# Moving one MLP step behind a division, and two v loads from slot 6 to slot 8

## The chip, the cores and the metric

The kernel runs on one core of one Trainium2 chip. Times are microseconds (us) on the device, from the first to the last instruction and what lies around them. A core has five engines that run beside each other, each in its own fixed order: PE (TensorE, matmuls; its weight loads are shown as PEld), DVE (VectorE), ACT (ScalarE), POOL (GpSimd) and SP (SyncE, which here only issues transfers). POOL issues the loads that also convert from 32 to 16 bits; SP issues stores, on-chip copies and DMA transposes. All transfers run on the same 16 DMA engines.

## The reference

Two stages. First a causal attention with a forget gate, 8 batches of 8 heads, 576 rows, head width 64; then an MLP of 512 to 2048 to 512 on all 4608 rows, with g = h - tanh(h) between.

```
scores = scale * np.matmul(q, k.transpose(0, 1, 3, 2))
log_f = np.log(np.clip(f, 0.0001, 1.0))
cum = np.cumsum(log_f, axis=-1)
decay = cum[:, :, :, None] - cum[:, :, None, :]
scores = np.where(causal, -1000000000.0, scores + decay)
attn = np.exp(scores - np.max(scores, axis=-1, keepdims=True))
attn = attn / (np.sum(attn, axis=-1, keepdims=True) + 1e-09)
x = np.matmul(attn, v) ...   # heads put side by side: (4608, 512)
h = x @ w_in
out = (h - np.tanh(h)) @ w_out
```

## The kernel before

**Order.** Every engine executes the program's order as it is written; no scheduler moves anything. The attention runs by pairs of heads, 4 pairs in each of the 8 batches. Batch 0 is written out by hand by blocks of 128 rows (0 to 3, and block 4 of 64 rows). From batch 1 on, a loop runs over slots: slot p (from 4) is the pair p of the list of (batch, pair), so slots 4 to 7 are batch 1, 8 to 11 batch 2, 12 to 15 batch 3. A slot has 7 tiles of scores. Between the tiles stand the loads of LOADS, keyed by (slot, tile), the transposes of TRANS, and, after tile 1, the value matmuls and the division of the pair of the slot before. MLP steps are put between these as filler for PE: `step()` emits the next one from a list. The first 13 are first-layer steps of unit 0, which are 8 matmuls of 256 columns each (L468), a tanh on ACT (L434) and an add on DVE (L435).

**Batch 0, by hand.** `scores0(ib, ti)` makes one tile of scores of block ib (L319, L322) and its exponential on ACT (L324); the score tiles use two PSUM banks in turn, so a tile waits for the exponential of the last but one. `values0(ib, halves)` multiplies the exponentials with v (L334). `norm0(ib)` divides on DVE (L343 to L345). `turn0(ib)` transposes the divided block on PE (L354) and copies it to XR (L355), where the MLP reads it. `trans(1, 0, qn, QT)` and `trans(1, 0, kn, KT)` transpose batch 1's first q and k on PE (L262) and copy them, half on ACT (L269) and half on DVE (L271). Steps, block 3's transpose and k's transposes share three further PSUM banks in turn.

**Loads.** `load_v(b, n)` (L94) loads block n of batch b's v, for all heads, into `vn[b % 2]`. `load_heads` (L105) loads block n of q or k of a batch from 3 on into a raw buffer; `turn_all` then transposes the whole raw buffer into TQ or TK with one DMA transpose on SP (L108), and `place` (L112) copies it to QT or KT. `weight_sums` (L458) are sums of parts of w_out for a fast product of the later units; the second group is written into raw q's buffer after TQ has read it. Each mask of a score tile is a select on POOL (L397), in the same queue as the loads, and the value matmuls (L406) wait for the masks. `load_wout` (L211) loads w_out in four parts. The loads on POOL use eight semaphores in turn: a load waits until the eighth load before it has landed.

**Who reads what.** Batch 2's v is read first by the values of its first pair, in slot 9 after tile 1. TQ of batch 3 is issued at (8, 4), TK at (9, 4), and batch 3's scores begin in slot 12.

Of the kernel before, what the change touches and what calls it, by code (L numbers as in the profile page):

```python
# [17 lines left out]
FAR = 3  # L18
# [4 lines left out]
def kernel(  # L23
# [54 lines left out]
    raw = [[qkp.tile([P, RW], FP16, tag=f"{x}n{i}", name=f"{x}n{i}") for i in range(2)] for x in "qk"]  # L78
# [13 lines left out]
    def load_block(dst, src, b, n, h0=0, h1=H):  # L92
        pn = min(P, S - n * P)
        nc.gpsimd.dma_start(out=dst[0:pn, n, h0:h1, 0:D], in_=src[b, h0:h1, n * P:n * P + pn, :].rearrange("h p d -> p h d"))  # L94
# [6 lines left out]
    def load_heads(dst, src, b, n):  # L101
        pn = min(P, S - n * P)
        to = dst[0:pn, n * P:n * P + D]
        to = bass.AP(to.tensor, to.offset, [list(to.ap[0]), [HP, H], [1, D]])
        nc.gpsimd.dma_start(out=to, in_=src[b, :, n * P:n * P + pn, :].rearrange("h p d -> p h d"))  # L105

    def turn_all(dst, src):
        nc.sync.dma_start_transpose(out=dst.rearrange("p (x t) -> p x t", t=P), in_=src[:, 0:TC])  # L108

    def place(dst, src, b, a):  # L110
        of = src[a * D:(a + 1) * D, a * LEAD:a * LEAD + NPAIR * PITCH].rearrange("d (c s) -> d c s", s=PITCH)
        nc.sync.dma_start(out=dst[b % 2][0:D, a:H:2, 0:S], in_=of[:, :, 0:S])  # L112

    def load_v(b, n):
        load_block(vn[b % 2], v, b, n)

    def raw_of(b):
        return 1 if b == FAR else 0
# [50 lines left out]
    def load_aug(b):  # L169
        i, h0 = b % 2, b * H  # L170
        nc.sync.dma_start(out=KT[i][D:D + 1, :, 0:S], in_=chi[h0:h0 + H, :])
        nc.sync.dma_start(out=QT[i][D + 2:D + 3, :, :], in_=cq[h0:h0 + H, :])
        nc.sync.dma_start(out=KT[i][D + 1:D + 2, :, 0:S], in_=clo[h0:h0 + H, :])
# [40 lines left out]
    def load_qk(dst, src, b, h0, h1):  # L214
        nc.gpsimd.dma_start(
            out=dst[b % 2][:, h0:h1, :, :].rearrange("p h n d -> p h (n d)"),
            in_=src[b, h0:h1, :, :].rearrange("h (p n) d -> p h (n d)", n=NT6))

    LOADS = {(NPAIR, 5): [lambda: load_qk(qn, q, 2, 0, HH)],
             (NPAIR + 1, 2): [lambda: load_qk(kn, k, 2, 0, HH)],  # L220
             (NPAIR + 1, 4): [lambda: load_qk(qn, q, 2, HH, H)],
             (NPAIR + 1, 6): [lambda: load_qk(kn, k, 2, HH, H)]}
# [6 lines left out]
    for b in range(2, B):  # L229
        p0 = (b - 1) * NPAIR  # L230
        for n in range(NJ):
            LOADS.setdefault((p0 + (2 if b == 2 else 1), n), []).append(lambda b=b, n=n: load_v(b, n))
        LOADS.setdefault((p0, 0), []).append(lambda b=b: load_aug(b))
        if b < FAR:
            continue
        for n in range(NJ):
            LOADS.setdefault((p0 - 1, n), []).append(lambda b=b, n=n: load_heads(raw[0][raw_of(b)], q, b, n))
            LOADS.setdefault((p0, n), []).append(lambda b=b, n=n: load_heads(raw[1][raw_of(b)], k, b, n))
        LOADS.setdefault((p0, 4), []).append(lambda b=b: turn_all(TQ, raw[0][raw_of(b)]))
        LOADS.setdefault((p0 + 1, 4), []).append(lambda b=b: turn_all(TK, raw[1][raw_of(b)]))  # L240
        for n, (dst, src) in enumerate(((QT, TQ), (KT, TK))):
            for a in range(2):
                LOADS.setdefault((p0 + 1 + n, 5 + a), []).append(lambda b=b, dst=dst, src=src, a=a: place(dst, src, b, a))
# [9 lines left out]
    def trans(b, c, src, dst, eng):  # L253
        pn, g3 = S // NT6, NT6 // 2
        if src is kn and (b, c) <= (2, 0):
            t32 = ps_m.tile([P, UW], FP32, tag="m", name="t32")
        else:
            t32 = ps_tr.tile([P, UW], FP32, tag="tr", name="t32")
        t16 = t32.bitcast(FP16)[:, 0:2 * S // 2].rearrange("p (a g n) -> p a g n", a=2, g=g3)
        for a in range(2):  # L260
            for g in range(g3):
                nc.tensor.transpose(out=t16[:, a, g, :],  # L262
                                    in_=src[b % 2][:, 2 * c + a, 2 * g:2 * g + 2, :],
                                    identity=id16[0:pn, 0:pn])
        for e in range(2):
            to = dst[b % 2][0:D, 2 * c:2 * c + 2, e:S:2].rearrange("d a (p g) -> d a p g", g=g3)
            of = t16[e * D:(e + 1) * D, :, :, :].rearrange("d a g p -> d a p g")
            if eng[e] == "A":
                nc.scalar.activation(out=to, in_=of, func=AF.Copy)  # L269
            else:  # L270
                nc.vector.tensor_copy(out=to, in_=of)  # L271
# [39 lines left out]
    def scores0(ib, ti):  # L311
        w = min(P, S - ib * P)
        n = UW // w
        ps = ps_sc.tile([P, 512], FP32, tag="sc", name="ps")
        e = aex.tile([P, 512], FP16, tag="e", name="e")
        todo = [(h, j) for h in range(H) for j in range(ib + 1)][n * ti:n * ti + n]
        for i, (h, j) in enumerate(todo):
            at = slice(i * w, (i + 1) * w)
            nc.tensor.matmul(out=ps[:, at], lhsT=KT[0][:, h, j * P:(j + 1) * P],  # L319
                             rhs=QT[0][:, h, ib * P:ib * P + w], start=True, stop=(j < ib))  # L320
            if j == ib:
                nc.tensor.matmul(out=ps[:, at], lhsT=neg16, rhs=tri16[:, 0:w], start=False, stop=True)  # L322
            E[(0, h, j, ib)] = e[:, at]
        nc.scalar.activation(out=e, in_=ps, func=AF.Exp, scale=qscale)  # L324

    def values0(ib, halves=(0, 1)):
        w = min(P, S - ib * P)
        if ib not in AV:
            av = ps_av.tile([P, 2, 512], FP32, tag="av", name="av")
            AV[ib] = av[0:w, :, 0:HH * (D + 1)].rearrange("p i (h d) -> p i h d", h=HH)  # L330
        av = AV[ib]
        for h in [a * HH + x for a in halves for x in range(HH)]:
            for j in range(ib + 1):
                nc.tensor.matmul(out=av[:, h // HH, h % HH, :], lhsT=E.pop((0, h, j, ib)),  # L334
                                 rhs=vn[0][:, j, h, 0:D + 1], start=(j == 0), stop=(j == ib))

    def norm0(ib):
        w = min(P, S - ib * P)
        av = AV.pop(ib)
        xn = fin.tile([P, NJ, P], FP16, tag="xn", name="xn")  # L340
        XN[(0, ib)] = xn[0:w, 0:NPAIR, :]
        rs = fin.tile([P, 2, HH, 1], FP32, tag="rs0", name="rs")[0:w]
        nc.vector.tensor_scalar_add(out=rs, in0=av[:, :, :, D:D + 1], scalar1=1e-9)  # L343
        nc.vector.reciprocal(out=rs, in_=rs)
        nc.vector.tensor_tensor(out=XN[(0, ib)].rearrange("p (i c) (a d) -> p i (c a) d", i=2, a=2),  # L345
                                in0=av[:, :, :, 0:D], in1=rs.to_broadcast([w, 2, HH, D]), op=ALU.mult)

    def turn0(ib):
        w = min(P, S - ib * P)
        xn = XN.pop((0, ib))  # L350
        x32 = ps_m.tile([P, UW], FP32, tag="m", name="x32")
        xt = x32.bitcast(FP16)[:, 0:NPAIR * w].rearrange("p (c n) -> p c n", c=NPAIR)
        for c in range(NPAIR):
            nc.tensor.transpose(out=xt[:, c, :], in_=xn[:, c, :], identity=id16[0:w, 0:w])  # L354
        nc.vector.tensor_copy(out=XR[:, :, ib * P:ib * P + w], in_=xt)  # L355
# [262 lines left out]
    def step(n=1):  # L618
        for fn, *args in mlp[done[0]:done[0] + n]:
            fn(*args)  # L620
        done[0] += n
# [132 lines left out]
    for _, two in raw:  # L754
        rows = two[3 * P // 4:P, 0:TC].rearrange("p (s d) -> p s d", d=D)
# [7 lines left out]
    scores0(3, 7)  # L763
    values0(3, (0,))
    scores0(4, 0)
    step()
    scores0(4, 1)
    values0(3, (1,))
    norm0(3)
    scores0(4, 2)  # L770
    trans(1, 0, qn, QT, "AV")
    turn0(3)
    scores0(4, 3)
    trans(1, 0, kn, KT, "AV")
    scores0(4, 4)
    step()
# [38 lines left out]
```

## Time and profile before

| what | us |
|---|---|
| median of 3 runs | 343.23 |
| lowest and highest of them | 342.43 and 344.86 |
| the profiled execution | 341.56 |
| its span, first to last instruction | 339.8 |
| DVE busy in the span | 238.3 (70%) |
| ACT busy | 226.5 (67%) |
| POOL busy | 162.2 (48%) |

The profile is one execution, recorded instruction by instruction. Busy times of different engines overlap. A matmul's recorded length includes the time that it takes to pass through the array, so one starts before the last has ended, and a busy PE can still lose time: the starts tell more than the lengths. L and a number is a line of the kernel; `out<-in` names what an instruction writes and reads; `x8` says that eight like it stand together. The landing of a transfer is the time at which its semaphore has its full count. The largest groups of POOL's loads on the page:

```profile
vn<-in_v_dram POOLq DMA_DIRECT2D x32, 128.0 KB, 6.9
...
qn<-in_q_dram POOLq DMA_DIRECT2D x24, 128.0 KB, 5.9
kn<-in_k_dram POOLq DMA_DIRECT2D x24, 128.0 KB, 4.4
```

(count, size, median us from issue to landing). In the slots of the change, slot 6 runs from about 46.5 us, slot 7 from 53, slot 8 from 60.5, slot 9 from 70 and slot 10 from 80.

### The profile page before, as it was taken

The page shows a single profiled execution, that of the slowest core. Times are in us where ns is not written, and L with a number is a line of the kernel's source. Part 1 is how long each engine was busy: PE and PEld are TensorE (multiplying, and loading weights), DVE is VectorE, ACT ScalarE, POOL GpSimd, SP SyncE. Part 2 cuts the span into 40 slices and gives each one's busy share as a digit, 9 for nine tenths or more (in the row PEclk, how much of TensorE's full clock was granted, in tenths as well). Part 3 has the DMA queues.
Part 4 walks back from the last instruction along what each step waited for, and adds up shares of the span by engine and source line. Part 5 has one row for each costly group of instructions (what it writes and reads, how often), then busy time and mean ns, then how long its engine had stood idle before and what let it go on. Part 6 is the DMA issues. An engine that isn't in the chain of part 4 may idle for free.

```text
span 339.8 us, 8818 instructions
## 1 busy us (share of the span) xinstructions
PE 330.9 (97%) x3405; PEld 237.8 (70%) x3405; DVE 238.3 (70%) x492; ACT 226.5 (67%) x424; POOL 162.2 (48%) x324
## 2 busy tenths in 40 slices
PE   7898999999999999999999999999999999999995
PEld 4887876655588558888885578657877786486484
DVE  7777884748985886478845885588547865974973
ACT  5787877778855886488557865787568734624731
POOL 8978387853466727772786358652222210000000
PEclk9999999999999999999999999999999999999999
DMA  9999999999999999999999999997230013012002
GB/s 85 148 195 185 206 190 166 178 150 208 189 134 113 207 207 126 154 229 180 152 133 207 183 155 158 196 179 172 62 112 19 20 50 110 1 33 93 2 31 93
DMA packets 162955, 45.96 MB, mean 135 GB/s; under 512 B 141602, under 2 KB 162402, under 8 KB 162914
## 3 DMA queue, kind: packets, MB, share of 16 engines
q0 software_dynamic: 101248, 18.36, 77.3%
q1 hardware_dynamic: 61586, 26.99, 39.1%
q8 instruction: 26, 0.43, 0.5%
q14 instruction: 15, 0.12, 0.1%
q10 hardware_dynamic: 80, 0.07, 0.1%
HBM read 36.85 MB, written 9.44 MB: 136 GB/s over the span
## 4 chain that ended last, share of the span: by engine, by line
PE 79%; DMA 11%; POOL 6%; issue 1%; DVE 1%; ACT 1%; POOLq 0%; ACTq 0%
PE hps L482 30%; PE cx L523 17%; PE cz L523 12%; PE ps L378 10%; PE av L406 7%; DMA wout<-in_moe_w_out_dram 5%; DMA vn<-in_v_dram 4%; PE ops L601 3%; DMA win<-in_moe_w_in_dram 2%; POOL vn L94 2%; POOL kn L98 1%; POOL qn L98 1%; POOL wout L211 1%; PE hps L468 1%; PE t L262 0%
## 5 line engine op out<-in xcount | busy, mean ns | idle before, releaser
L435 DVE TENSOR_TENSOR gt<-hps,th 128x512 f16<-128x512 f32 x144 | 98.7, 689 | 44.0 <-ACT th L434 42.9
L482 PE MATMUL hps<-XR,win 128*128 128x512 f16 (+4 forms) x640 | 125.8, 336 | 0.4 <-DVE gt L435 0.4
L387 ACT ACTIVATE e<-ps 128x512 f16<-128x512 f32 x168 | 98.4, 595 | 34.4 <-PE ps L378 33.2
L434 ACT ACTIVATE th<-hps 128x512 f32<-128x512 f32 x144 | 86.1, 598 | 28.0 <-PE hps L482 19.9
L397 POOL TENSOR_SCALAR_AFFINE_SELECT e<-e 128x128 f16<-128x128 f16 x162 | 55.1, 342 | 100.8 <-ACT e L387 100.4
L482 PEld LDWEIGHTS <-win 128*128 128x128 f16 x640 | 56.3, 97 | 43.8 <-issue 0.6
L378 PE MATMUL ps<-QT,KT 67*128 67x512 f16 (+1 forms) x336 | 68.6, 277 | 0.4 <-ACT e L387 0.3
L523 PEld LDWEIGHTS <-gt 128*128 128x128 f16 x640 | 59.9, 97 | 9.5 <-DVE gt L435 0.4
L378 PEld LDWEIGHTS <-KT 67*128 67x128 f16 x336 | 32.0, 98 | 18.8 <-issue 1.0
L94 POOL DMA_DIRECT2D vn<-in_v_dram x40 | 34.4, 861 | 5.8 <-DMA win<-in_moe_w_in_dram 2.2
L516 DVE TENSOR_TENSOR snap<-cz,snap 128x512 f32<-128x512 f32 x24 | 16.6, 691 | 23.1 <-ACT e L387 10.1
L523 PE MATMUL cz<-wout,gt 128*128 128x256 f16 x256 | 32.0, 272 | 0.0
L406 PEld LDWEIGHTS <-e 128*128 128x128 f16 x784 | 28.2, 97 | 3.7 <-POOL e L397 0.2
L406 PE MATMUL av<-vn,e 128*128 128x65 f16 x784 | 29.6, 193 | 0.1
L523 PEld LDWEIGHTS <-sw 128*128 128x128 f16 x256 | 24.0, 97 | 4.5
L523 PE MATMUL cx<-kn,gt 128*128 128x256 f16 x192 | 25.7, 273 | 0.0
L414 DVE TENSOR_TENSOR xn<-av,rs 128x640 f16<-128x640 f32 x28 | 23.1, 825 | 1.0
L105 POOL DMA_DIRECT2D qn<-in_q_dram x25 | 21.3, 852 | 1.7 <-issue 1.3
L105 POOL DMA_DIRECT2D kn<-in_k_dram x25 | 21.3, 852 | 1.2 <-issue 1.2
L560 ACT ACTIVATE snap<-cx 128x512 f32<-128x512 f32 (+1 forms) x18 | 9.9, 549 | 16.6 <-PE cx L523 16.6
L324 ACT ACTIVATE e<-ps 128x512 f16<-128x512 f32 x25 | 14.5, 596 | 4.4 <-PE ps L322 2.3
L468 PE MATMUL hps<-XR,win 128*128 128x256 f16 x128 | 16.6, 273 | 0.3 <-DVE gt L435 0.3
(113 smaller groups left out, 372.0 us busy)
## 6 DMA issues: line engine op xcount, KB each, us to landing
vn<-in_v_dram POOLq DMA_DIRECT2D x32, 128.0 KB, 6.9
out_dram<-snap SPq DMA_DIRECT2D x16, 256.0 KB
qn<-in_q_dram POOLq DMA_DIRECT2D x24, 128.0 KB, 5.9
kn<-in_k_dram POOLq DMA_DIRECT2D x24, 128.0 KB, 4.4
QT<-TQ SPq DMA_DIRECT2D x10, 288.0 KB
KT<-TK SPq DMA_DIRECT2D x10, 288.0 KB
out_dram<-ost SPq DMA_DIRECT2D x11, 256.0 KB
win<-in_moe_w_in_dram POOLq DMA_DIRECT2D x4, 512.0 KB, 8.2
```

Source lines behind the costliest of these rows:

```text
L94: nc.gpsimd.dma_start(out=dst[0:pn, n, h0:h1, 0:D], in_=src[b, h0:h1, n * P:n * P + pn, :].rearrange("h p d -> p h d"))
L105: nc.gpsimd.dma_start(out=to, in_=src[b, :, n * P:n * P + pn, :].rearrange("h p d -> p h d"))
L378: nc.tensor.matmul(out=ps[:, col:col + n], lhsT=KT[b % 2][0:D + 3, h, j * P:(j + 1) * P], rhs=QT[b % 2][0:D + 3, h, i0:i0 + n], start=True ...
L387: nc.scalar.activation(out=e[:, lo:hi], in_=ps[:, lo:hi], func=AF.Exp, scale=qscale)
L397: nc.gpsimd.affine_select(out=view, in_=view, compare_op=ALU.is_ge, fill=0.0, base=0, pattern=pat, channel_multiplier=-1)
L406: nc.tensor.matmul(out=av[:, a, ib, :], lhsT=E.pop((b, 2 * c + a, j, ib)), rhs=vn[b % 2][:, j, 2 * c + a, 0:D + 1], start=(j == 0), stop=( ...
L414: nc.vector.tensor_tensor(out=xn.rearrange("p i (a d) -> p a i d", a=2), in0=av[:, :, :, 0:D], in1=rs.to_broadcast([P, 2, NJ, D]), op=ALU. ...
L434: nc.scalar.activation(out=th, in_=hps, func=AF.Tanh, scale=-1.0)
L435: nc.vector.tensor_tensor(out=to, in0=view(hps), in1=view(th), op=ALU.add)
L468: nc.tensor.matmul(out=hps[:, w * SB:(w + 1) * SB], lhsT=win[:, ci, ft * P:(ft + 1) * P], rhs=XR[:, ci, t * SB:(t + 1) * SB], start=(ci == ...
L482: nc.tensor.matmul(out=hps[:, o:o + n], lhsT=win[:, ci, ft * P:(ft + 1) * P], rhs=XR[:, ci, t:t + n], start=(ci == 0), stop=(ci == NCH - 1))
L523: nc.tensor.matmul(out=ps, lhsT=stationary(u, LHS[ph], ft, m), rhs=moving(RHS[ph], ft), start=fresh and ft == 0, stop=(ft == HF - 1), skip ...
```

## The change

In batch 0's hand-written end, the second MLP step moves from behind the first score tile of block 4 to behind block 3's division, and block 3's transpose goes one score tile later. In LOADS, batch 2's five v blocks, before at tiles 0 to 4 of slot 6, go to tiles 0, 2 and 4 of slot 6 and tiles 0 and 1 of slot 8; batch 3's five k blocks, before at tiles 0 to 4 of slot 8, go to tiles 2 to 6. All other loads keep their tiles. The number of instructions on each engine is the same; SP's order is the same.

```diff
     for n in range(NJ):
-            LOADS.setdefault((p0 + (2 if b == 2 else 1), n), []).append(lambda b=b, n=n: load_v(b, n))
+            at = ((p0 + 2, 0), (p0 + 2, 2), (p0 + 2, 4), (p0 + 4, 0), (p0 + 4, 1))[n] if b == 2 else (p0 + 1, n)
+            LOADS.setdefault(at, []).append(lambda b=b, n=n: load_v(b, n))
...
         for n in range(NJ):
-            LOADS.setdefault((p0 - 1, n), []).append(lambda b=b, n=n: load_heads(raw[0][raw_of(b)], q, b, n))
-            LOADS.setdefault((p0, n), []).append(lambda b=b, n=n: load_heads(raw[1][raw_of(b)], k, b, n))
+            for x, (rows, src) in enumerate(((raw[0], q), (raw[1], k))):
+                at = 7 * (p0 - 1 + x) + n + (2 * x if b == FAR else 0)
+                LOADS.setdefault(divmod(at, 7), []).append(
+                    lambda b=b, n=n, rows=rows, src=src: load_heads(rows[raw_of(b)], src, b, n))
...
     scores0(4, 0)
-    step()
     scores0(4, 1)
     values0(3, (1,))
     norm0(3)
+    step()
     scores0(4, 2)
     trans(1, 0, qn, QT, "AV")
+    scores0(4, 3)
     turn0(3)
-    scores0(4, 3)
     trans(1, 0, kn, KT, "AV")
```

## The prediction

> **What bounds the kernel now.** I read first the page's busy shares and its 40 slices, for the engine that sets the time.
>
> ```profile
> PE 330.9 (97%) x3405; PEld 237.8 (70%) x3405; DVE 238.3 (70%) x492; ACT 226.5 (67%) x424; POOL 162.2 (48%) x324
> ...
> PE   7898999999999999999999999999999999999995
> ...
> PEclk9999999999999999999999999999999999999999
> ```
>
> TensorE is busy 330.9 of 339.8 us at the full granted clock (0.998). The change adds and removes no instruction, so it can only touch the stretches in which PE does not issue. The starts of successive matmuls, less each one's own length, show which stall is worth how much. From 8 us on, three belong to the places of the diff: 1.30 us at 27.35, 0.42 us in two pieces at 54.6 and 55.0, and 0.53 us at 86.96. After 96 us none is over 0.12 us. Next I read the waits, whose columns are the waiter, who ended the wait, us in total, times and longest:
>
> ```profile
> POOL vn L94 <- DMA wout<-in_moe_w_out_dram: 1.2, 1, 1.2
> ...
> PE x L354 <- DVE xn L345: 1.1, 1, 1.1
> ...
> DVE qn L458 <- DMA TQ<-qn: 0.7, 1, 0.7
> ```
>
> Last, the timeline around each (start, length, engine, line; in brackets the idle time before it and what ended it). The first place is the end of batch 0:
>
> ```profile
> 23.37 0.60 ACT L324 ACTIVATE e<-ps 128x512 f16<-128x512 f32 x1
> ...
> 23.86 1.04 PE L468 MATMUL hps<-XR,win 128*128 128x256 f16 x8
> 24.73 0.22 PE L319 MATMUL ps<-QT,KT 67*128 67x64 f16 x2
> ...
> 25.04 0.65 PE L334 MATMUL av<-vn,e 128*128 128x65 f16 x16
> ...
> 25.79 0.42 PE L262 MATMUL t<-id,qn 96*128 96x96 f16 x6
> ...
> 26.60 0.69 DVE L345 TENSOR_TENSOR xn<-av,rs 128x512 f16<-128x512 f32 x1
> ...
> 27.35 0.40 PE L354 MATMUL x<-id,xn 128*128 128x128 f16 x4 [1.14 <-DVE xn L345]
> ```
>
> PE finishes its transposes at 26.2 and stands until DVE has divided block 3 (26.60 + 0.69 = 27.29); only then can turn0(3) run. The second place is slot 6:
>
> ```profile
> 46.77 0.58 PE L406 MATMUL av<-vn,e 128*128 128x65 f16 x14
> ...
> 52.42 0.89 POOL L94 DMA_DIRECT2D vn<-in_v_dram  x1 [1.23 <-DMA wout<-in_moe_w_out_dram]
> ...
> 53.33 0.30 POOL L397 TENSOR_SCALAR_AFFINE_SELECT e<-e 128x128 f16<-128x128 f16 x1
> ...
> 53.57 0.69 POOL L94 DMA_DIRECT2D vn<-in_v_dram  x1
> ...
> 54.26 0.90 POOL L397 TENSOR_SCALAR_AFFINE_SELECT e<-e 128x128 f16<-128x128 f16 x3
> ...
> 54.39 1.03 PE L406 MATMUL av<-vn,e 128*128 128x65 f16 x14
> ```
>
> POOL's loads use eight semaphores in turn, so each waits for the eighth before it. Batch 2's fourth v block waits for the last quarter of w_out (issued 34.85, landed 51.52). Behind it on POOL stand the masks of tiles 4 to 6, so the value matmuls of the next slot, 14 of which took 0.58 us a slot earlier, take 1.03. The third place is slots 8 to 10:
>
> ```profile
> 68.56 5.66 SPq L108 DMA_TRANSPOSE TQ<-qn  x1
> ...
> 80.33 0.43 DVE L458 TENSOR_TENSOR qn<-wout,t 128x512 f16<-128x512 f16 x1 [0.74 <-DMA TQ<-qn]
> ...
> 86.96 1.02 PE L482 MATMUL hps<-XR,win 128*128 128x512 f16 x4 [0.36 <-DVE gt L435]
> ```
>
> The turn of batch 3's q (TQ) can start only when its loads have landed (last one 68.43, issue 68.56). It lands at 80.2, and DVE, which must overwrite that buffer, stands 0.74 us and then runs without a gap until PE waits for it at 86.96.
>
> **Part one, the step and the turn.** The step is 8 matmuls, 0.87 us of PE (23.86 to 24.73). Taken out there, the tile scores0(4,1) comes 0.87 us earlier, too early: its PSUM bank (two in turn) is held by the exponential of tile (3,7) until 23.37 + 0.60 = 23.97. The restart takes about 0.05 us (the like wait before 34.15 us ended 0.05 after its exponential), so a new stall of 0.16; bounds 0, if that wait is hidden, and 0.44, the stall at 34.15. I take 0.16, from the rows themselves. Adding the issue lengths: scores (4,1) 24.02 to 24.33, values 0.48 to 24.81, step to 25.68, scores (4,2) 0.27, transposes 0.25, scores (4,3) 0.31, to 26.51. The division starts 0.1 after the values' last matmul ends (25.0) and needs what it needed before (26.17 to 27.29, 1.12): 26.2. So turn0(3) at 26.51 waits for nothing, and ends at 26.74; the k transposes end at 26.99. Scores (4,4) need the exponential of (4,2), now behind the step's tanh on ACT: tanh 25.91 to 26.51, exponential to 27.0. That is 0.05 lost. Step 3 then starts at 27.35, before at 28.44: **1.09 us earlier** (1.30 less 0.16 and 0.05).
>
> Queued behind the moved pieces: on DVE the step's gate add now follows the division and ends at about 27.25, just before step 3 needs its bank, a margin of 0.1. Block 3's copy into XR goes behind the QT copy, to about 28.9, and the next user of its bank comes at 29.7. On ACT the last exponential of block 4 moves from 29.30 to about 28.8; the last eight value matmuls want it at 29.4 and it ends at 29.4. If all three margins fail together, some 0.3 us is lost. Nothing is issued on SP or POOL by this part.
>
> **Part two, the loads.** Two POOL instructions (0.89 and 0.69 us) leave slot 6, two masks move up, and the third v block and all of batch 3's q come earlier. The eighth load before the new slot 7's first is now the last w_out quarter, reached at about 52.7, after its landing: the 1.23 us wait goes. Masks 5 and 6 of slot 6 are then done by about 52.2, before the values (53.93 less 1.09 = 52.84) want them: **0.42 us gained.** Nothing else is late there: PE's own next wait on that quarter, the matmuls at 53.07, comes 1.09 earlier at 51.98, 0.46 after the landing.
>
> In slot 8 POOL has seven loads where it had five: 7 x 0.86 + 7 x 0.33 = 8.3 us in a slot of 9.5 (61.9 to 71.4). The masks wait on the exponentials there (idle 0.99 and 0.40 before the last ones), so the two loads take idle time; without that cover they would cost 0.89 + 0.69 = 1.6 us at the next values. The loads on POOL's queue land back to back, 768 KB from 60.87 to 68.43. Taking 192 KB out ahead of q leaves 576 KB, 5.7 us: q's last lands at about 66.5, SP is free of the XR transposes at 67.08 - 1.5 = 65.6, and TQ starts at 66.6, 2.0 us earlier; its landing goes from 80.2 to about 78.3. DVE comes to its overwrite at 79.59 - 1.5 = 78.1. The stall of 0.74 shrinks to about 0.2 and with it PE's 0.53: **0.4 us gained**, bounds 0 and 0.53.
>
> The v blocks now fetched in slot 8 are issued at about 60.2 and 61.9 and come behind q in the queue: landed by about 68.4, or 69.4 if the XR transposes slow the queue as they did at 69 to 70 us (55 KB in that us, 115 usual). The values of batch 2 want them at about 72.2 - 1.5 = 70.7. [...]
>
> Batch 3's k lands some 2 us later, at about 75.5 (67.76 to 73.94 before), its turn TK starts by SP's order at about 76.6, and K is placed at 94 us where slot 12 wants it at 99: free.
>
> Sum: 1.1 + 0.4 + 0.4 = 1.9 us. The profiled execution took 341.56 us (span 339.8 and 1.8 around it), so it would take 339.7. It lies 1.67 below the median of the three runs, 343.23, to which I apply the same gain: 341.3.
>
> **Rivals.** *The transfers cap it.* PE runs earlier, the queues do not: if the last w_out quarter lands at 52.5 instead of 51.52 because the XR transposes also come earlier, or TQ lands at 80.2 as before, the lead shrinks. Against it: the queue was already backlogged from 30 us. For it: TQ would now run beside the k loads, where before it moved its bytes from 73 to 77 us, when k had landed. Only half the sum would be left, 0.3 to 1.2: 342.5. [...]
>
> *The v blocks come late*, the side that is slower. PE's values of batch 2 stand at 70.7 until block 4 lands, and everything is behind them. It decides from 70.7 on, and cancels the gain at 72.6. The worst v load of the trace took 11.8 us: 61.9 + 11.8 = 73.7, a stall of 3.0 less the gain of 1.9 is 1.1 slower, 344.3. Against it: that load was issued at 46.95 behind the w_out backlog.
>
> *It does nothing:* the exponentials' two banks take back at (4,1) and (4,4) what the fill gave, 0.44 each as at 34.15, and slot 8's masks take the rest: 343.2. The rows above leave it little.
>
> **How the numbers follow.** Forecast 0.60, transfers cap it 0.22, v late 0.10, nothing 0.08. The forecast's own width is 1.2 to 2.2 by the bounds above, and the three runs of before span 2.4 us, so a median wanders by some 0.7. That gives 340.0 to 343.4, which takes in the cap and nothing and leaves out the late half of the v rival. A measurement of this kernel tells about 1% from no change, 3.4 us; the forecast is 0.6%. Over 1% faster 0.06, from the wander; slower by over 1% needs v blocks after 76 us: 0.04; within 0.90.
>
> **What would show it.** Right: PE's wait for xn at L354 gone and step 3 at 27.3; no wait of POOL's on wout; values of slot 7 at 0.6 us; TQ issued before 67.5; no DVE wait for TQ at L458. Wrong: PE waiting at the values near 70 us for v, or a DVE wait of over 1 us for TQ. A new stall over 0.5 us between 23 and 30 us would break part one.

## The result, and the profile after

The changed kernel took 345.37 us (median of 22 runs, 342.86 to 490.85), the kernel before 342.7 in the same session (22 runs, 341.0 to 345.78). The ratio is 1.0066 (95%: 1.0042 to 1.0090): 0.66% slower, where 0.6% faster was forecast. A second set of 12 runs, e1_both below, gave 344.27 and 1.0029 (1.0001 to 1.0057). The highest of the 22 runs, and the one that was profiled with them, were disturbed and are left out of the ratio, so the profile read here is that of e1_both, the same kernel: its profiled execution took 346.76 us with a span of 345.1, against 341.56 and 339.8 before. It lies 2.5 us above the median of its 12 runs, and the profiled execution of before 1.1 us below 342.7, so a median run probably loses less than what is read below.

The page of the changed kernel first, busy shares and slices:

```profile
PE 332.8 (96%) x3405; PEld 238.8 (69%) x3405; DVE 238.5 (69%) x492; ACT 226.2 (66%) x424; POOL 163.0 (47%) x324
...
PE   7999998996999999999999998999999999999995
...
PEclk9999999998999999999999999999999999999999
```

PE still sets the time, but its slices have three new dents (the 8 at about 52 us, the 6 at about 82 us and the 8 at about 211 us), and the clock row, all 9 before, has an 8 in the same slice as the second. The waits of this profile (waiter, who ended the wait, us in total, times, longest) name them:

```profile
DVE qn L461 <- DMA TQ<-qn: 3.8, 1, 3.8
...
PE hps L485 <- DVE gt L438: 2.7, 1, 2.7
...
POOL qn L105 <- DMA wout<-in_moe_w_out_dram: 1.2, 1, 1.2
```

The wait for xn at the turn is gone, DVE's wait for TQ is 3.8 us where it was 0.74, and POOL still stands 1.2 us for w_out, now in front of a q load. (The lines below the diff have moved down by three: L354 is now L357, L458 is L461, L435 is L438, L482 is L485.) The timeline shows the three places of the prediction in turn. The end of batch 0 (start, length, engine, line; idle time before it in brackets):

```profile
24.25 0.65 PE L337 MATMUL av<-vn,e 128*128 128x65 f16 x16
...
24.73 1.04 PE L471 MATMUL hps<-XR,win 128*128 128x256 f16 x8
...
25.37 0.69 DVE L348 TENSOR_TENSOR xn<-av,rs 128x512 f16<-128x512 f32 x1
...
26.43 0.39 PE L357 MATMUL x<-id,xn 128*128 128x128 f16 x4
...
27.24 1.04 PE L471 MATMUL hps<-XR,win 128*128 128x256 f16 x8
```

The division ends at 26.06 and its transposes start at 26.43 with no bracket: PE did not wait. Step 3 starts at 27.24; 27.35 was predicted, 28.44 was before. The second place, slot 6 and the start of 7:

```profile
50.52 0.89 POOL L94 DMA_DIRECT2D vn<-in_v_dram  x1 [0.29 <-DMA wout<-in_moe_w_out_dram]
...
52.30 0.29 POOL L400 TENSOR_SCALAR_AFFINE_SELECT e<-e 128x128 f16<-128x128 f16 x1 [0.21 <-ACT e L390]
...
52.92 1.02 PE L604 MATMUL ops<-wout,gt 128*128 128x512 f16 x4 [0.89 <-DMA wout<-in_moe_w_out_dram]
53.78 0.59 PE L409 MATMUL av<-vn,e 128*128 128x65 f16 x14
```

The masks are done by 52.6 and the values take 0.59 us, as forecast; but just ahead of them PE stands at the matmuls that read w_out's last quarter, which landed at 52.88 in this execution. The third place:

```profile
68.91 7.98 SPq L108 DMA_TRANSPOSE TQ<-qn  x1
...
83.33 0.42 DVE L461 TENSOR_TENSOR qn<-wout,t 128x512 f16<-128x512 f16 x1 [3.80 <-DMA TQ<-qn]
...
84.41 1.86 PE L485 MATMUL hps<-XR,win 128*128 128x512 f16 x4 [2.73 <-DVE gt L438]
```

TQ goes out at 68.91 and takes SP 7.98 us to issue (5.66 before), lands at 83.21 (80.21 before), and DVE stands in front of its overwrite. Behind the overwrite on DVE are the gate adds that free PE's banks, so PE stands too. The four matmuls after that stall take 1.86 us instead of 1.02: the clock. The windows of this profile say so (us, then busy time and count of PE, PEld, DVE, ACT, POOL, then granted clock, DMA share, GB/s):

```profile
80.80:84.20 3.40, 0.88 (x6) 0.39 (x4) 0.87 (x2) 0.71 (x2) 0.29 (x1) 1.00 2.04 184
84.20:87.60 3.40, 3.19 (x32) 2.08 (x32) 3.34 (x7) 1.68 (x3) 0.29 (x1) 0.50 1.60 200
```

By the starts of matmuls (the eight at 23.86 of before are recorded as 1.04 us, and the next one starts 0.87 after them), PE loses at the places of the change 0.16 at 23.95, 1.05 at 52.92, 0.57 in two pieces near 72 (values waiting for a v block), 2.89 at 84.41 and 0.80 by the halved clock: 5.47 us, where it was 1.30 + 0.42 + 0.53 = 2.25. That is 3.2 of the 5.2 us between the spans (345.05 and 339.85). Another 1.43 is one wait for a K of a later batch at 211 us, which none of the other twelve profiles has there; the rest, about 0.6, is no more than the later start of the full clock allows (5.7 us instead of 4.1, worth up to 0.8: in the profile of before, matmuls of 512 columns start 0.43 us apart ahead of it, and 0.21 apart behind it in the groups of four that take 1.02 us).

### The profile page after: what moved, and what is told of

Same layout as the page of the kernel before. It is cut to its first block, busy times and chain, and to the rows that moved or that the text cites. A ratio compares the mean times of both kernels' runs of the same rounds, so it can differ in the third digit from the quotient of the medians.

```text
span 380.3 us, 8818 instructions
## 1 busy us (share of the span) xinstructions
PE 374.7 (99%) x3405; PEld 257.3 (68%) x3405; DVE 242.5 (64%) x492; ACT 227.5 (60%) x424; POOL 162.3 (43%) x324
## 3 DMA queue, kind: packets, MB, share of 16 engines
q0 software_dynamic: 101248, 18.36, 66.7%
## 4 chain that ended last, share of the span: by engine, by line
PE 98%; ACT 1%; DVE 0%; issue 0%; ACTq 0%
PE hps L485 34%; PE cx L526 17%; PE cz L526 13%; PE ps L381 12%; PE av L409 7%; PE hps L471 4%; PE ops L604 4%; PE ps L322 2%; PE t L265 1%; PE spin L253 1%; PE av L337 1%; PE t L294 1%; PE ps L325 0%; ACT e L327 0%; PE t L280 0%; PE x L357 0%
## 5 line engine op out<-in xcount | busy, mean ns | idle before, releaser
L485 PE MATMUL hps<-XR,win 128*128 128x512 f16 (+4 forms) x640 | 143.6, 370 | 0.0
L438 DVE TENSOR_TENSOR gt<-hps,th 128x512 f16<-128x512 f32 x144 | 99.5, 691 | 63.2 <-ACT th L437 61.4
L390 ACT ACTIVATE e<-ps 128x512 f16<-128x512 f32 x168 | 98.3, 594 | 44.2 <-PE ps L381 37.7
L485 PEld LDWEIGHTS <-win 128*128 128x128 f16 x640 | 60.9, 104 | 53.4
L381 PE MATMUL ps<-QT,KT 67*128 67x512 f16 (+1 forms) x336 | 75.5, 302 | 0.0
L526 PEld LDWEIGHTS <-gt 128*128 128x128 f16 x640 | 64.7, 105 | 14.1
L381 PEld LDWEIGHTS <-KT 67*128 67x128 f16 x336 | 34.7, 106 | 23.2 <-issue 0.2
L526 PE MATMUL cz<-wout,gt 128*128 128x256 f16 x256 | 36.2, 295 | 0.0
L526 PE MATMUL cx<-kn,gt 128*128 128x256 f16 x192 | 29.0, 296 | 0.0
L471 PE MATMUL hps<-XR,win 128*128 128x256 f16 x128 | 18.7, 295 | 0.0
L604 PE MATMUL ops<-wout,gt 128*128 128x512 f16 x64 | 18.7, 420 | 0.0
## 6 DMA issues: line engine op xcount, KB each, us to landing
out_dram<-snap SPq DMA_DIRECT2D x16, 256.0 KB
out_dram<-ost SPq DMA_DIRECT2D x11, 256.0 KB
```

The source lines that it names most:

```text
L381: nc.tensor.matmul(out=ps[:, col:col + n], lhsT=KT[b % 2][0:D + 3, h, j * P:(j + 1) * P], rhs=QT[b % 2][0:D + 3, h, i0:i0 + n], start=True ...
L390: nc.scalar.activation(out=e[:, lo:hi], in_=ps[:, lo:hi], func=AF.Exp, scale=qscale)
L438: nc.vector.tensor_tensor(out=to, in0=view(hps), in1=view(th), op=ALU.add)
L471: nc.tensor.matmul(out=hps[:, w * SB:(w + 1) * SB], lhsT=win[:, ci, ft * P:(ft + 1) * P], rhs=XR[:, ci, t * SB:(t + 1) * SB], start=(ci == ...
L485: nc.tensor.matmul(out=hps[:, o:o + n], lhsT=win[:, ci, ft * P:(ft + 1) * P], rhs=XR[:, ci, t:t + n], start=(ci == 0), stop=(ci == NCH - 1))
L526: nc.tensor.matmul(out=ps, lhsT=stationary(u, LHS[ph], ft, m), rhs=moving(RHS[ph], ft), start=fresh and ft == 0, stop=(ft == HF - 1), skip ...
```

## The experiments

Each kernel had 12 runs and stood against 35 runs of the kernel before in its job (medians 343.11, 343.12 and 342.16). "The second group" below is the four parts of the sums of w_out that DVE writes into raw q's buffer after TQ has read it.

**e1_both: the change again, for its trace.**

> The changed kernel again, for a profile at the full clock. Measured so far: 0.66% slower (2.3 us). Theory L (the loads lose it): the profile shows a stall of 2 us or more between 65 and 100 us that before did not have. Theory P (the hand-written end loses it): step 3 starts later than before's 28.44. Theory C (the clock): no stall is new, and the granted clock begins later or is lower.

Measured: 344.27, ratio 1.0029 (1.0001 to 1.0057); the profile is the one above. Slower a second time, and the gain at 27 us is real in the same profile, so it is lost elsewhere.

**e2_end_only: the step and the turn alone.** Against the changed kernel it puts the loads back (it is the kernel before with the end moved, and has the line numbers of before):

```diff
-at = ((p0 + 2, 0), (p0 + 2, 2), (p0 + 2, 4), (p0 + 4, 0), (p0 + 4, 1))[n] if b == 2 else (p0 + 1, n)
+at = (p0 + (2 if b == 2 else 1), n)
-at = 7 * (p0 - 1 + x) + n + (2 * x if b == FAR else 0)
+at = 7 * (p0 - 1 + x) + n
```

> Only the step and the turn moved, loads as before. Theory L: 1.1 us faster (0.3%), wait for xn gone. Theory P: 2 us slower, as both together. Theory C: as both together if the clock follows from PE standing less in the beginning.

Measured: 343.15, ratio 0.9992 (0.9961 to 1.0022). No gain, although the scores that were at 34.15 us in the profile of before come at 32.71. Its timeline in slot 7:

```profile
52.67 1.02 PE L601 MATMUL ops<-wout,gt 128*128 128x512 f16 x4 [0.88 <-DMA wout<-in_moe_w_out_dram]
...
53.54 0.89 POOL L94 DMA_DIRECT2D vn<-in_v_dram  x1 [2.50 <-DMA wout<-in_moe_w_out_dram]
...
54.80 0.23 PE L406 MATMUL av<-vn,e 128*128 128x65 f16 x2 [0.65 <-POOL e L397]
...
55.73 0.80 PE L406 MATMUL av<-vn,e 128*128 128x65 f16 x12 [0.69 <-POOL e L397]
```

w_out's last quarter (landed 52.63) stops PE itself for 1.04 by the starts, and POOL in front of a v load, behind which the masks are late: another 1.93 at 54.8 to 56.1, against 0.42 before. What PE was early by, it waits here for a transfer that does not come earlier. The masks' 1.93 do not come from the end: e4 below has the end of before and the same 1.93. This execution also lost the full clock behind these stalls (its mean clock is 0.995).

**e3_loads_only: the loads alone,** the last part of batch 0 as before:

```diff
 scores0(4, 0)
+step()
 scores0(4, 1)
 values0(3, (1,))
 norm0(3)
-step()
 scores0(4, 2)
 trans(1, 0, qn, QT, "AV")
-scores0(4, 3)
 turn0(3)
+scores0(4, 3)
```

> Only the loads moved, the hand-written end as before. Theory L: 2 to 3.5 us slower. Theory P: 0.4 to 0.8 us faster. Theory C: within 0.5 us of before.

Measured: 345.13, ratio 1.0028 (0.9996 to 1.0059). The masks' stall is gone here too, and TQ is as late as in e1:

```profile
69.13 7.83 SPq L108 DMA_TRANSPOSE TQ<-qn  x1
...
83.49 0.42 DVE L461 TENSOR_TENSOR qn<-wout,t 128x512 f16<-128x512 f16 x1 [4.04 <-DMA TQ<-qn]
...
84.57 1.87 PE L485 MATMUL hps<-XR,win 128*128 128x512 f16 x4 [2.96 <-DVE gt L438]
```

This ratio alone is not clear of noise, as its interval reaches below 1; but the stall is the same as in e1, so the end is not needed for it, and e5 below puts the loss on the loads.

**e4_k_later_only and e5_v_later_only: each half of the loads.** Both have the end of before. e4 moves batch 3's k to tiles 2 to 6 and leaves v in slot 6; e5 moves v and leaves k at tiles 0 to 4:

```diff
 # e4, against before
-LOADS.setdefault((p0, n), []).append(lambda b=b, n=n: load_heads(raw[1][raw_of(b)], k, b, n))
+LOADS.setdefault(divmod(7 * p0 + n + (2 if b == FAR else 0), 7), []).append(lambda b=b, n=n: load_heads(raw[1][raw_of(b)], k, b, n))
 # e5, against before
-LOADS.setdefault((p0 + (2 if b == 2 else 1), n), []).append(lambda b=b, n=n: load_v(b, n))
+at = ((p0 + 2, 0), (p0 + 2, 2), (p0 + 2, 4), (p0 + 4, 0), (p0 + 4, 1))[n] if b == 2 else (p0 + 1, n)
+LOADS.setdefault(at, []).append(lambda b=b, n=n: load_v(b, n))
```

> Only batch 3's k two tiles later; batch 2's v stays in slot 6. Theory L splits: if the late k loads (running beside TQ) lose the time, 2 us slower as with all loads moved; if the v blocks in slot 8 lose it, same as before within 0.5 us. Theories P and C: same as before.

> Only batch 2's v moved (slot 6 and 8), batch 3's k back at tiles 0 to 4 of slot 8. Theory T (TQ lands late because POOL's loads run beside it, and DVE stands before it overwrites TQ's source): with k two tiles earlier, fewer loads run beside TQ; TQ lands by 81 to 82 against 83.3, DVE stands 1.5 to 2.5 us against 3.9, time 0.5 to 1.5 us below the two moves together. Rival (v itself late at the values of slot 9): a PE stall at the values near 70 us, and no less time.

Measured: e4 342.51, ratio 0.9987 (0.9958 to 1.0015); e5 344.59, ratio 1.0056 (1.0030 to 1.0081). The v blocks alone make the kernel slower, k alone does nothing that shows. So what was expected of e5 did not come: with k back at its tiles TQ is in the air as long as in e1 (14.3 us), DVE stands 2.9 us, and no time is gained, while the rival's stall at the values is there, 0.52 us by the starts:

```profile
67.95 7.35 SPq L108 DMA_TRANSPOSE TQ<-qn  x1
72.14 0.19 PE L407 MATMUL av<-vn,el 128*128 128x65 f16 x1 [0.35 <-DMA vn<-in_v_dram]
82.34 0.42 DVE L459 TENSOR_TENSOR qn<-wout,t 128x512 f16<-128x512 f16 x1 [2.90 <-DMA TQ<-qn]
```

**e6_both_t2_later and e7_before_t2_later: the second group written later,** so that DVE comes to the buffer after TQ; e6 on the changed kernel, e7 on the one before.

```diff
-(q0 + 1, 5), (q0 + 2, 1), (q0 + 2, 3), (q0 + 2, 5),
+(q0 + 2, 3), (q0 + 2, 4), (q0 + 2, 5), (q0 + 2, 6),
```

> The changed kernel, and the second group of weight sums, which overwrites TQ's source, four to six tiles later (slot 10, tiles 3 to 6), with the same work. Theory T: DVE's stand of 3.9 us at 79.5, PE's stall of 2.9 at 84.4 and the clock's drop behind it go; 3 to 4.5 us faster than the changed kernel, 1 to 2 faster than before. Rival (the loads or the clock cost it otherwise): within 1 us of the changed kernel.

> The kernel before with the same later weight sums, as a control. Theory T: only before's own stand of DVE (0.7 to 1.5 us) and PE's stall of about 0.5 to 1.2 go: 0.5 to 1 us faster than before. If it gains as much as the changed kernel with later sums, the sums alone are the gain and the moved loads bring nothing.

Measured: e6 342.23, ratio 0.9965 (0.9932 to 0.9998); e7 342.0, ratio 0.9985 (0.9953 to 1.0017). In e6 TQ is as slow as ever (67.65 to 81.73), but its overwrite stands at 86.14 and waits for nothing:

```profile
86.14 0.44 DVE L461 TENSOR_TENSOR qn<-wout,t 128x512 f16<-128x512 f16 x1
```

The edit is worth 0.64% on the changed kernel (1.0029 in e1 to 0.9965, and the intervals do not meet) and 0.15% on the one before, within its interval. What makes the change slow is thus mainly DVE's wait for TQ, not TQ's lateness as such. e6's next stall is 0.89 us at 98.06, for K's placement.

**e8_both_step_swap: a first-layer step ahead of the matmuls that need w_out's last quarter,** to give back the end's gain:

```diff
-for j in ((0,), (1,), (), ())[i]
+for j in ((0, 1), (), (), ())[i]
```

> The changed kernel with one first-layer step moved ahead of the second-layer steps that need w_out's last quarter. Theory W (the hand-written end does gain 1.1 us, and PE gives it back at 52.9 waiting for that quarter): the stall of 1.05 at 52.9 falls below 0.3 and 0.7 to 1.1 us are gained up to slot 8; since DVE then stands longer for TQ, little of it is left at the end. Rival (the end gains nothing): no stall there goes, slot 7 starts at the same time.

Measured: 343.41, ratio 1.0013 (0.9981 to 1.0046). The 1.05 us at w_out are gone from its trace, the stall for TQ is still there (2.59 us), and the values of slot 9 wait 1.06 us for v blocks. The gain up to slot 8 came in the trace: its first values of slot 7 start at 53.16 against 53.78 in e1, although it was 0.38 us behind e1 at 42 us. The difference from e1 in the whole time, 0.16%, is inside the intervals.

**e9_both_v3_later: batch 3's v blocks out of TQ's way,** one slot later:

```diff
-... if b == 2 else (p0 + 1, n)
+... if b == 2 else (p0 + (2 if b == 3 else 1), n)
```

> The changed kernel, with batch 3's five v loads one slot later (slot 10), out of TQ's flight; weight sums where they were. Theory T (POOL's loads beside TQ slow it): TQ lands 10 to 12 us after its issue against 14.3, DVE's stand of 3.9 us falls below 2, PE's stall of 2.9 below 1.2, 1 to 2.5 us faster than the changed kernel. Rival (TQ is slow for another reason, such as the k loads alone or SP): still 13.5 to 14.5 us, no gain.

Measured: 341.53, ratio 0.9973 (0.9943 to 1.0003).

```profile
67.94 7.97 SPq L108 DMA_TRANSPOSE TQ<-qn  x1
...
79.08 0.42 DVE L461 TENSOR_TENSOR qn<-wout,t 128x512 f16<-128x512 f16 x1 [1.07 <-DMA TQ<-qn]
```

TQ lands 11.0 us after its issue instead of 14.3, with the two moved v blocks still in slot 8, and DVE and PE stand less, as expected of theory T. The ratio is 0.56% below e1's, with intervals that just meet. SP's issue time stays at 7.97: six loads are out when TQ is issued, as in e1, but one and not five follow in the next 8 us. Between these two profiles, then, the loads that follow lengthen the landing and not the issue.

**e10_both_t2_swap, e11_end_t2_later, e12_loads_t2_later: the parts again, with the second group later.** e10 has e6's and e8's edits on the changed kernel, e11 the end alone with e6's edit, e12 the loads alone with it.

> The changed kernel with the later weight sums and the swapped step together: both waits that took the gain are gone. Sum of the theories: 1.1 us from the hand-written end kept, 0.4 from the masks, 0.5 to 1 from the sums, so 1.5 to 2.5 us faster than before, and 0 to 1 us faster than with the later sums alone. Rival: as with the later sums alone.

> The hand-written end alone with the later weight sums. If the end's 1.1 us is given back to w_out's last quarter and the masks wait longer: same as before with later sums, 342.0, within 0.7 us, with a stall at 52 to 56 us 1 us larger than that one's. Rival: 1.1 us faster than it.

> The moved loads alone with the later weight sums. If their whole loss went through the wait for TQ: 0.3 to 0.8 us faster than before with later sums, since the masks' stall near 55 us (0.4 to 0.8) is gone. If v also comes late at slot 9's values: as that one or up to 0.5 slower, with 0.2 to 0.7 us lost near 72 us.

Measured: e10 341.41, ratio 0.9966 (0.9934 to 0.9997); e11 342.58, 1.0010 (0.9981 to 1.0038); e12 340.47, 0.9961 (0.9930 to 0.9992). With DVE's wait away, the moved loads no longer cost anything: e12's windows where e1 has its hole show PE full and the clock whole. Whether they gain is not shown: the later sums alone gave 0.15% (e7), and the 0.24% from there to e12 are inside the intervals.

```profile
80.00:84.00 4.00, 4.00 (x48) 2.37 (x46) 3.87 (x9) 2.83 (x6) 0.63 (x2) 1.00 1.77 195
84.00:88.00 4.00, 4.00 (x23) 1.92 (x22) 4.00 (x9) 3.84 (x9) 1.17 (x4) 1.00 1.38 157
```

The end shows no gain in this company either (e11; e6 against e12), and e10's swap adds nothing to e6 that shows. e10's profiled execution stood 4.73 us for K's placement at 101.8, so its stretch after that is not compared. e12, e6 and e10 are faster than the kernel before by 0.34 to 0.39%, with intervals that end just below 1.

## Why the prediction was wrong, step by step

**"Step 3 then starts at 27.35 ... 1.09 us earlier": right, at its own place.** The order of the rows, the 0.16 stall at 23.95 and the start (27.24) came as worked out; e1 and e2 have the scores of 34.15 at 32.95 and 32.71.

**"PE's own next wait on that quarter ... 0.46 after the landing": wrong, and with it part one's gain in e1 and e2.** It took one landing of the profile of before, 51.52, as fixed. In the profiles here that quarter landed from 51.4 to 53.3 us, whatever was done to the end: 52.88 in e1, 52.63 in e2, 53.27 in e11, 51.91 in e9. PE now arrives at about 52, inside that range, so what is left of the end's 1.09 us depends on the landing: 1.05 are waited away in e1, 1.04 in e2 and more in e11, but only 0.36 in e9, and nothing in e6, where it landed at 51.72. The rival that the transfers cap it named this spot and priced it at 52.5. Both its issue (34.0 to 36.1) and its flight (16.7 to 18.2) scatter; the cause of that stays open, and each kernel was traced in one execution only.

**"Masks 5 and 6 ... 0.42 us gained": right** in e1 and e3, and low if anything: with the v blocks in slot 6 the masks cost 0.42 us before, 0.78 in e7 and 1.93 in e2, e4 and e11. **"The 1.23 us wait goes": wrong,** it is 1.19 us, in front of a q load. No stall of PE follows it, but with two like it (0.55 and 0.97 us, for k loads) it keeps q's last load at 60.37, where it was at 60.33 before.

**"TQ starts at 66.6, 2.0 us earlier; its landing goes from 80.2 to about 78.3": the step that failed.** It started at 68.91 and landed at 83.21. The start: taking 192 KB out ahead of q was to bring q's last landing from 68.43 to 66.5, but it came at 68.76. The third v block, ahead of it, landed at 64.42 instead of 60.87: the queue had already fallen behind at w_out. Over the profiles the start did come earlier on the whole, at 66.7 to 69.1 us with the v blocks moved and at 67.8 to 70.5 with them in slot 6, so it is the flight that failed. The flight: I kept the 11.7 us of before, although the text itself said that TQ would run beside the k loads; it measured 14.3 in e1. Counting POOL's loads (128 KB each, every fifth of a tensor 64 KB) that are still out when TQ is issued or are issued within 8 us after it, the traces give:

| profile | loads beside TQ | issue to landing, us |
|---|---|---|
| e2, end only | 7 | 8.5 |
| e9, batch 3's v later | 7 | 11.0 |
| before; e7 | 8; 8 | 11.7; 10.6 |
| e4, k later; e11 | 9; 9 | 11.9; 10.8 |
| e5, v later | 10 | 14.3 |
| e12; e10 | 10; 10 | 12.7; 14.4 |
| e1; e3; e6; e8 | 11 each | 14.3; 14.2; 14.1; 13.7 |

That is about 1.1 us a load (an estimate, from a line through the table), though equal counts differ by up to 2.5 us: 8 loads go with 10.6 to 11.7 us, 11 with 13.7 to 14.3, and three more loads cost 3 us. It is the moved v blocks that push the rest of the queue into TQ's flight: they alone give the 14.3 (e5), the moved k alone 11.9 (e4). The DMA rows show the sharing: from 73 to 77 us the queue that carries TQ and SP's other transfers moved 0.66 MB in the profile of before, beside under 0.01 MB of POOL's; in e1 it moved 0.34 MB, beside 0.12 MB of POOL's. In e9, four fewer loads beside TQ than in e1 took 3.3 us off. How the queues share the engines no row here shows. The cap rival was right that TQ would run beside POOL's loads, but its price of 342.5 was too low: it let TQ land "at 80.2 as before" at worst.

**"The stall of 0.74 shrinks to about 0.2": wrong in sign,** 3.80 in e1. PE's stall went from 0.53 to 2.89, and the halved clock behind it, which the prediction had in no case, is 0.80 more. Both things that the prediction named as signs of being wrong came: this wait of over 1 us for TQ, and PE waiting for v.

**"Landed by about 68.4, or 69.4": wrong,** 71.77 and 72.19 in e1; that is the rival of the late v blocks, at a price of 0.57 us (0.25 in e3, 0.52 in e5, 1.06 in e8, none in e6, e9 and e12), below its own 3.0.

**K "free": not always.** It was placed at 98.1 in e1 (94.8 before), and e6 lost 0.89 us to it, e10's traced execution 4.73.

**The range and the chances.** The sign was wrong and the time outside the range; that the change is within 1% was right. 0.6 went to a forecast that needed three transfers to come at the times of one trace.

## What to carry to other kernels

A transfer's duration in a trace belongs to what was in the air beside it (TQ took 8.5 us beside 7 loads in e2, 14.3 beside 11 in e1): before moving loads, list what will be out during each long transfer that something waits for, and price the added ones. A gain ahead of a landing ends at that landing, so ask how much the landing scatters (51.4 to 53.3 us here) before counting a margin of half a microsecond. Where an engine waits in order for a buffer to be read (DVE here), moving that one overwrite behind other work can be worth more (0.64% on the changed kernel, in e6) than making the read earlier.

## What was unexpected of the hardware

**The clock fell after a stall of under 3 us, and not every time.** In e1 TensorE was busy 0.88 of 3.4 us (80.8 to 84.2), and then had half its clock for 3.41 us. The full clock lasted 78.5 us ahead of that stretch and 256.0 us behind it. e3 shows the same at 84.0 with a stall of 3.13 us (mean clock 0.995, and four matmuls of 512 columns in 1.87 us behind it instead of 1.02); e8, with 2.59, and e5, with 1.99, show none in their profiles (mean clock 1.000 and 0.999). The length of the longest stall alone does not decide it: 2.73 us idle was enough in e1, and e2 lost the clock at 56.8 after stalls of 1 us at most that left PE busy for 1.96 of the 3.4 us before. What does decide it is not shown here.

**It can be counted without a trace.** One such stretch lowers a run's mean clock by half of 3.4 us in 345, to 0.995, which is what the profiled runs of e2 and e3 have, and those of e6, e8 and e11, without one, 1.000. Of the runs of the changed kernel that enter the ratios, 22 of 32 have a clock under 0.998; of before's, 9 of 102; e12 has none of 11, e6 2 of 11, e9 2 of 12. Runs under it are longer by 1.3 us in the median in both sets of the changed kernel (345.57 and 344.25; 345.05 and 343.72). By that share, (0.69 - 0.09) x 1.3 = 0.8 us of the 1.2 to 2.7 us by which its medians lie above before's go with the runs that lost the clock. That is an estimate of the two together: a run that loses the clock may also be one with a longer stall, and the runs without a trace cannot tell.

**The issue of a DMA transpose is not a constant:** the same TQ held SP for 4.38 us in e2 and 7.98 in e1.
